# Distances added to the scores by TensorE in the first half of batch 0, in place of mask products, with a new order of steps

## The chip, the cores and the metric

The kernel runs on one core of a Trainium2 chip. A core has a matrix engine (TensorE), VectorE, ScalarE, GpSimd and a queue engine (SyncE, "SP"), which work beside each other and are tied together by semaphores, and 16 DMA engines that all queues share. TensorE writes to PSUM, which has eight banks; the other engines read it from there. The metric is the device time of one execution in microseconds (us). A profile is one execution of its own; its "span" reaches from the first instruction to the last.

## The reference

Attention over 4 batches, 8 heads, 768 positions of 64 values, with 8 global keys and a local band of 96, and distances with a slope for each head as bias; then a gated feed-forward layer over the 3072 tokens:

```python
scores = scale * np.matmul(q, k.transpose(0, 1, 3, 2))
is_global = pos[None, :] < int(n_global)
is_local = (rel >= 0) & (rel < int(n_local))
keep = is_global | is_local
dist = np.where(is_global & ~is_local, float(n_local), np.abs(rel).astype(np.float32))
slopes = 2.0 ** (-8.0 * (np.arange(H, dtype=np.float32) + 1) / H)
bias = -slopes[:, None, None] * dist[None, :, :]
scores = np.where(keep, scores + bias[None, :, :, :], -1000000000.0)
a = np.exp(scores - max); a = a / (sum(a) + 1e-09)
x = np.matmul(a, v)                  # then tokens x 512
g = x @ w_gate
out = (g / (1 + exp(-g)) * (x @ w_val)) @ w_out
```

(The lines are joined and shortened.) `w_gate` and `w_val` are 512 x 1536, `w_out` is 1536 x 512.

## The kernel before

All matrix operands are 16-bit floats; loads on GpSimd's queue narrow them on the way from HBM.

Attention. The keys are cut into 14 chunks of 56, each with the 8 global keys in front (64 rows); a chunk is met by a window of 152 queries. Chunks are packed into "units": in batch 0 units 0 and 1 cover the first 384 queries, units 2 to 4 the second 384; in the other batches five units cover all 768. A unit has two groups of four heads (g = 0, 1); TensorE works on four heads at a time, each in a 64 x 64 quarter of its array. For batch 0, q and k are loaded by halves (`ld_half`, a load of 96 KB each for two head pairs), turned by matmuls with an identity (`tr_half`), and copied out of PSUM (`keys_half`, `queries_half`). Then for each unit and group:

- `scores` (step `c`): k times q into two PSUM banks;
- `exps` (`x`): the exponential, on ScalarE;
- `mask` (`m`): on VectorE, a product with the exponential of slope times distance, which is zero where a key is not to be seen. These masks are made by `make_masks` (`M`) from a small table `dist` of three window patterns.

When the units of a half are ready, `weigh` (`w`) sums the exponentials (part 0) and multiplies them with v (parts 1 and 2); `invert` (`i`) and `spread_r` (`r`) make the reciprocals of the sums, and `scaled` (`p`) writes x, transposed, for 384 tokens, in two sides. Batch 1's q and k come partly by `ld_four` (`L4`) and matmuls (`U`), partly, as in batches 2 and 3, by `ld_rows` (`Lr`), DMA transposes on SP's queue (`tr_dma`, `D`) and copies (`K`).

v is loaded head by head with `ld_v` (`Lv`). In batch 0 each head has two loads, one for chunks 0 to 6 and one for 7 to 12. Batch 0's global rows of v are loaded once (`VG`), narrowed (`Ga`) and copied to every chunk (`Gc`).

Feed-forward. The 3072 tokens are eight blocks of 384. For each block and each of 12 column blocks f: four products with `w_gate` (`g`) and four with `w_val` (`v`), a hyperbolic tangent on ScalarE (`t`), two VectorE steps (`s`, `h`), and then the output products (`o`) with `w_out`, copied out and stored (`e`) through SP's queue. The weights come in pieces of 256 KB (`Lw.which.n.c`: gate or value, four column blocks f, half of the rows).

The order. Nothing is scheduled by a compiler: `ORDER` is a list of some 2,000 steps, written out, and each engine and each queue meets its part of it in that order. `fill.N@bank` are matmuls of ones into an unused bank; they compute nothing. `name@bank` gives the PSUM bank. GpSimd issues nearly all loads and has at most eight in flight.

Of the kernel before, what the change touches and what calls it, by code (L numbers as in the profile page):

```python
# [21 lines left out]
def _build_dist(NG, NL, H):  # L22
# [20 lines left out]
    d = np.concatenate([np.concatenate([d, d]), slopes.reshape(2 * CH, 4)], axis=1)  # L43
# [16 lines left out]
Lw.1.1.1 ga.0.0@0 x.0.1.2 Lv.0.6.7.13 ga.0.1@1 gb.0.1 va.0.1@7 m.0.1.4.V t.0.1 va.0.0@6 Lw.1.1.0  # L60
vb.0.1 Lw.0.2.1 m.0.1.2.V m.0.1.3.V g.0.3@3 x.0.0.2 v.0.3@2 s.0.1 Lw.0.2.0 vb.0.0 v.0.2@4 t.0.3
h.0.1 m.0.0.2.V w.0.1.0@5 Lr.1.1.7 Lr.1.1.5 g.0.4@1 gb.0.0 g.0.2@7 t.0.4 Lr.1.1.1 D.1.3.1 s.0.3
h.0.3 Lr.1.1.3 i.0.1 r.0.1 Lw.1.2.1 L4.0.0 g.0.6@3 LG.1.1 U.2.0@2 s.0.4 U.3.0@5 t.0.0 s.0.0 g.0.7@1
g.0.5@0 t.0.2 s.0.2 Lw.1.2.0 Lo.0 t.0.6 Lr.1.1.4 h.0.0 Lr.1.1.2 h.0.2 s.0.6 w.0.1.1@6 Lr.1.1.6
w.0.1.2@3 kw.3.A t.0.5 v.0.4@5 p.0.1.0 v.0.6@6 LG.3.1 v.0.7@7 h.0.4 v.0.5@5 p.0.1.1 g.1.0@3 h.0.6
g.0.11@4 kw.2.V s.0.5 g.1.1@6 t.1.0 LG.2.1 s.1.0 Lo.1 g.1.4@0 D.1.2.1 h.0.5 g.1.6@2 Lr.1.1.0 Lo.2
t.0.11 t.1.4 Lv.1.2.0.13 Lr.2.0.3 v.1.4@3 g.1.5@5 s.0.11 s.1.4 t.0.7 s.0.7 h.0.7 g.0.10@0 v.1.5@4
t.1.5 t.1.1 s.1.5 h.1.4 s.1.1 v.1.0@1 t.0.10 Lt.2.0 g.1.10@7 h.1.0 U.0.0@3 h.1.5 U.1.0@5 kw.0.V
g.1.9@4 t.1.6 g.1.11@1 v.0.10@6 t.1.10 v.1.2@3 s.1.10 kw.1.V s.0.10 h.0.10 s.1.6 v.0.11@5 h.0.11
t.1.11 v.1.1@7 h.1.1 g.1.3@0 v.1.10@6 g.1.2@7 o.0.1.0@2 h.1.10 s.1.11 v.1.6@5 t.1.3 t.1.9 t.1.2  # L70
g.0.8@6 s.1.2 D.1.1.1 s.1.9 LG.1.0 g.0.9@1 t.0.9 h.1.6 h.1.2 v.0.9@7 LG.3.0 Lt.1.0 Lt.1.1
Lv.1.1.0.13 g.1.8@4 s.1.3 s.0.9 Lv.1.3.0.13 h.0.9 v.1.3@5 v.0.8@3 t.0.8 s.0.8 Lr.3.1.7 Lv.1.6.0.13
c.1.1.0@0 o.0.2.0@7 o.0.1.1 h.0.8 h.1.3 c.1.1.1@5 x.1.1.0 D.1.0.1 x.1.1.1 c.1.1.2@0 x.1.1.2 t.1.8
m.1.1.2.V s.1.8 o.0.1.2 m.1.1.1.V o.0.1.3 e.0.1 o.0.2.1 o.0.2.2 o.0.2.3 o.1.2.0@3 Lv.1.7.0.13
o.0.0.0@5 v.1.11@6 c.1.0.1@0 Lr.2.0.2 Lr.2.1.2 o.0.0.1 Lv.1.4.0.13 Lv.1.5.0.13 Lv.1.0.0.13 e.0.2
g.1.7@2 x.1.0.1 m.1.0.1.V m.1.1.0.V o.0.0.2 v.1.9@4 t.1.7 Lr.2.1.0 s.1.7 o.0.0.3 v.1.8@2 G.1.0 G.1.1
Lv.3.4.0.13 c.1.0.2@0 Lr.2.1.4 x.1.0.2 h.1.11 h.1.9 h.1.8 v.1.7@6 Lr.2.0.4 Lr.2.1.5 o.1.2.1
c.1.0.0@0 h.1.7 e.0.0 o.1.2.2 o.1.2.3 o.1.1.0@7 x.1.0.0 e.1.2 o.1.1.1 m.1.0.0.V o.1.1.2 m.1.0.2.V
o.1.1.3 w.1.0.0@4 Lr.2.0.0 Lr.3.0.0 w.1.0.1@5 w.1.0.2@0 i.1.0 r.1.0 o.1.0.0@2 Lr.3.0.2 p.1.0.1
o.1.0.1 e.1.1 o.1.0.2 Lr.2.1.1 o.1.0.3 e.1.0 c.1.0.4@3 x.1.0.4 c.1.0.3@0 p.1.0.0 c.1.1.4@5 g.2.5@7  # L80
x.1.1.4 x.1.0.3 g.2.0@3 t.2.5 m.1.1.4.V v.2.9@6 t.2.0 s.2.5 m.1.0.3.V g.2.9@0 g.2.2@5 Lr.2.1.3
Lr.2.0.6 v.2.5@4 LG.2.0 t.2.9 s.2.9 h.2.5 Lv.2.7.0.13 c.1.1.3@1 s.2.0 x.1.1.3 m.1.0.4.V m.1.1.3.V
g.2.3@7 Lr.2.0.1 h.2.9 g.2.8@0 v.2.3@4 D.2.0.0 w.1.1.0@2 i.1.1 Lr.2.1.6 g.2.1@3 g.2.7@6 v.2.1@1
t.2.3 s.2.3 D.2.2.1 D.2.1.1 t.2.1 s.2.1 t.2.2 s.2.2 Lv.3.2.0.13 Lt.3.1 h.2.1 Lr.3.1.3 Lr.2.1.7
Lr.2.0.7 g.2.4@7 h.2.3 g.2.6@3 v.2.2@1 r.1.1 D.2.1.0 G.2.1 v.2.0@2 g.2.10@5 t.2.6 Lr.2.0.5 h.2.2
s.2.6 v.2.8@4 v.2.4@3 t.2.4 h.2.0 K.2.0.A t.2.7 s.2.7 s.2.4 h.2.4 v.2.6@1 Lv.2.3.0.13 D.2.2.0
Lr.3.1.4 D.2.3.0 D.2.3.1 w.1.1.1@6 t.2.10 s.2.10 w.1.1.2@2 v.2.10@5 h.2.6 g.2.11@1 t.2.11 p.1.1.1
o.2.0.0@2 o.2.0.1 h.2.10 p.1.1.0 t.2.8 s.2.8 h.2.8 g.3.9@3 g.3.11@5 t.3.11 v.2.7@6 v.2.11@7 s.2.11
g.3.5@0 s.3.11 h.2.7 Lr.3.0.5 K.2.1.A t.3.9 Lv.2.2.0.13 Lv.2.0.0.13 Lv.3.7.0.13 o.2.0.2 t.3.5 h.2.11
Lr.3.1.0 o.2.0.3 v.3.11@4 g.3.7@5 D.2.0.1 o.2.1.0@7 g.3.2@1 o.2.2.0@6 o.2.2.1 K.2.2.A Lt.2.1 s.3.9  # L90
e.2.0 t.3.7 s.3.7 o.2.2.2 h.3.11 K.2.3.V o.2.2.3 t.3.2 s.3.5 c.2.1.2@4 Lr.3.0.1 s.3.2 c.2.0.0@2
c.2.0.1@0 x.2.1.2 e.2.2 Lv.2.5.0.13 Lv.2.1.0.13 m.2.1.2.V o.2.1.1 o.2.1.2 v.3.7@4 h.3.7 x.2.0.0
m.2.0.0.V g.3.0@5 x.2.0.1 o.2.1.3 t.3.0 c.2.1.0@2 x.2.1.0 m.2.1.0.V c.2.1.1@0 v.3.2@4 h.3.2 v.3.5@6
g.3.1@2 e.2.1 v.3.9@3 x.2.1.1 v.3.1@4 Lr.3.0.4 m.2.0.1.V t.3.1 s.3.1 v.3.0@1 h.3.9 Lv.3.3.0.13
g.3.3@0 t.3.3 Lr.3.0.7 Lv.2.6.0.13 g.3.10@7 h.3.5 Lr.3.1.5 s.3.0 c.2.0.2@2 c.2.1.3@5 h.3.1 t.3.10
# [38 lines left out]
def kernel(  # L134
# [95 lines left out]
    def v_of(b):  # L230
        return vSs[b % NV]
# [458 lines left out]
```

## Time and profile before

| what | value |
|---|---|
| device time, three runs | 241.59, 243.34, 243.68 us (median 243.34) |
| profiled execution | 241.13 us, span 239.2 us |
| granted TensorE clock, mean | 0.999 |
| ScalarE busy | 99.7 us (42%) |
| DMA, mean over the span | 106 GB/s |
| loads of `ld_half`, issue to landing, median | 5.6 us (k), 6.1 us (q) |

A line of the timeline reads: start, length, engine, line of the kernel, operation, what is written from what, how many instructions of the kind are merged, and in brackets how long the engine stood idle before and what ended that. Matmuls overlap, so the length of a group is the time from its first start to its last end. In the chain of waits a line has start, length and what the time went to; "issue" is time in which nothing in the profile was waited for. POOL is GpSimd, DVE is VectorE, ACT is ScalarE, PE is TensorE, PEld its weight loads.

### The profile page before, as it was taken

Reading aid. Unit: us, or ns where it says so; the run is one execution under the profiler, and the core shown is the slowest. Engines: PE = TensorE matmul, PEld = TensorE weight load, DVE = VectorE, ACT = ScalarE, POOL = GpSimd, SP = SyncE. Lnnn points to the kernel's source line nnn. Section 1 sums busy time; section 2 is a strip of 40 time slices with the busy share of each in tenths; the row PEclk is TensorE's granted clock in tenths of the full one; section 3 lists DMA queues with packets and bytes.
Section 4 is the critical chain, followed back from the end, with each engine's and each line's share of the span. In section 5 each row is a group of like instructions: output and inputs, shape, how many; then the busy total and the mean of one; then the engine's idle time right before and its main releaser. Section 6 shows DMA issues by size and latency. Waiting matters only on the chain.

```text
span 239.2 us, 7117 instructions
## 1 busy us (share of the span) xinstructions
PE 230.2 (96%) x3048; PEld 133.2 (56%) x3048; DVE 163.4 (68%) x362; ACT 99.7 (42%) x186; POOL 92.2 (39%) x123
## 2 busy tenths in 40 slices
PE   6897989999999999999999999999999999999994
PEld 4665556655445556555555556545665566545643
DVE  7389978987265688853996886894777366634840
ACT  5596443323542534447651328552333223222401
POOL 8798896645699990599800000000000000000000
PEclk9999999999999999999999999999999999999999
DMA  7999999999999999999991680003000210012003
GB/s 99 170 138 167 178 153 182 183 163 183 166 148 184 203 154 154 137 147 155 143 123 47 145 159 9 1 3 123 14 0 0 90 47 0 0 47 88 0 10 125
DMA packets 90767, 25.36 MB, mean 106 GB/s; under 512 B 78336, under 2 KB 87792, under 8 KB 90736
## 3 DMA queue, kind: packets, MB, share of 16 engines
q0 software_dynamic: 70128, 14.21, 68.8%
q1 hardware_dynamic: 20464, 10.58, 22.1%
q8 instruction: 24, 0.39, 0.7%
q10 hardware_dynamic: 144, 0.12, 0.2%
q14 instruction: 7, 0.06, 0.1%
HBM read 28.51 MB, written 6.29 MB: 145 GB/s over the span
## 4 chain that ended last, share of the span: by engine, by line
PE 84%; DMA 8%; POOL 5%; issue 1%; DVE 0%; POOLq 0%
PE PS L582 50%; PE PS L614 27%; PE PS L475 3%; PE PS L538 3%; DMA wg<-in_moe_w_gate_dram 3%; DMA st<-in_q_dram 3%; POOL vS L271 3%; DMA wv<-in_moe_w_val_dram 2%; PE PS L532 1%; POOL st L253 1%; POOL wv L319 1%; POOL wg L319 1%; PE PS L426 0%; DVE osb L623 0%; POOLq L670 0%
## 5 line engine op out<-in xcount | busy, mean ns | idle before, releaser
L588 ACT ACTIVATE th<-PS 128x384 f32<-128x384 f32 x96 | 44.4, 492 | 75.9 <-PE PS L582 70.6
L582 PE MATMUL PS<-xT,wv 128*128 128x384 f16 x384 | 72.4, 326 | 1.4 <-DMA wv<-in_moe_w_val_dram 1.4
L582 PE MATMUL PS<-xT,wg 128*128 128x384 f16 x384 | 73.2, 326 | 0.0
L614 PE MATMUL PS<-wo,hT 128*128 128x512 f16 (+2 forms) x300 | 67.9, 371 | 0.0
L599 DVE TENSOR_TENSOR hT<-PS,sl 128x384 f16<-128x384 f32 x96 | 51.2, 552 | 24.0 <-PE PS L582 22.2
L592 DVE SCALAR_TENSOR_TENSOR sl<-th,PS 128x384 f32<-128x384 f32 x96 | 50.7, 547 | 18.6 <-ACT th L588 17.9
L582 PEld LDWEIGHTS <-wv 128*128 128x128 f16 x384 | 37.1, 98 | 27.7 <-DMA wv<-in_moe_w_val_dram 1.9
L582 PEld LDWEIGHTS <-wg 128*128 128x128 f16 x384 | 36.5, 98 | 25.2 <-issue 0.2
L614 PEld LDWEIGHTS <-hT 128*128 128x128 f16 x300 | 28.0, 98 | 29.3
L484 ACT ACTIVATE at<-PS 128x912 f16<-128x912 f32 (+1 forms) x40 | 32.0, 829 | 20.8 <-PE PS L475 20.7
L271 POOL DMA_DIRECT2D vS<-in_v_dram x40 | 32.9, 834 | 8.4 <-DMA wo<-in_moe_w_out_dram 2.3
L505 DVE TENSOR_TENSOR at<-at,masks 128x912 f16<-128x912 f16 (+5 forms) x56 | 22.6, 442 | 13.0 <-ACT at L484 13.0
L629 ACT ACTIVATE osb<-PS 128x512 f32<-128x512 f32 (+1 forms) x24 | 14.2, 593 | 34.1 <-PE PS L614 31.6
L312 POOL DMA_DIRECT2D st<-in_q_dram x24 | 21.1, 885 | 1.5 <-DMA wv<-in_moe_w_val_dram 1.5
L312 POOL DMA_DIRECT2D st<-in_k_dram x16 | 13.9, 896 | 8.9 <-DMA kN<-st 8.8
L567 DVE TENSOR_TENSOR xT<-PS,rb 128x768 f16<-128x768 f32 x16 | 14.9, 951 | 1.8 <-PE PS L538 1.2
L475 PE MATMUL PS<-qT,kT 64*64 64x152 f16 (+4 forms) x464 | 12.4, 225 | 1.8 <-issue 1.0
L475 PEld LDWEIGHTS <-kT 64*64 64x64 f16 x464 | 8.0, 106 | 7.8 <-issue 6.4
L538 PEld LDWEIGHTS <-vS 64*32 64x32 f16 x1024 | 9.3, 90 | 3.4 <-issue 2.9
L538 PE MATMUL PS<-at,vS 64*32 64x152 f16 (+4 forms) x1024 | 10.5, 218 | 0.0
L358 PE MATMUL PS<-ones 128*128 128x256 f16 x44 | 8.8, 366 | 1.2 <-DVE ones L334 1.2
L556 DVE STREAM_TRANSPOSE rb<-dR 128x768 f32<-128x768 f32 x8 | 7.8, 976 | 0.2
(49 smaller groups left out, 95.9 us busy)
## 6 DMA issues: line engine op xcount, KB each, us to landing
out_dram<-osb SPq DMA_DIRECT2D x23, 256.0 KB, 2.5
st<-in_q_dram POOLq DMA_DIRECT2D x24, 96.0 KB, 6.1
vS<-in_v_dram POOLq DMA_DIRECT2D x24, 91.0 KB, 4.9
wv<-in_moe_w_val_dram POOLq DMA_DIRECT2D x6, 256.0 KB, 6.2
wg<-in_moe_w_gate_dram POOLq DMA_DIRECT2D x6, 256.0 KB, 6.5
wo<-in_moe_w_out_dram POOLq DMA_DIRECT2D x3, 512.0 KB, 10.0
st<-in_k_dram POOLq DMA_DIRECT2D x16, 96.0 KB, 5.6
st<-in_k_dram POOLq DMA_DIRECT2D x4, 192.0 KB, 6.5
```

Of the source, the lines that this page charges most:

```text
L271: nc.gpsimd.dma_start(out=v_of(b)[CH * c + NG:CH * c + CH, c0:c1, j, :], in_=v[b, h, KC * c0:KC * c1, :].rearrange("(i p) d -> p i d", p=KC))
L312: nc.gpsimd.dma_start(out=stage(b, i, h % 2, True)[:, h // 4, :, h // 2 % 2, :], in_=KQ[i][b, h].rearrange("(t p) d -> p t d", p=128))
L475: nc.tensor.matmul(PS[64 * e:64 * e + 64, bank + hi, col:col + n], lhsT=kT_of(b, hp)[r, CH * c:CH * c + CH], rhs=qTs[b, hp][r, q0:q0 + n], ...
L484: nc.scalar.activation(out=at[:, :, 0:w], in_=PS[:, bank:bank + 2, 0:w], func=AF.Exp, scale=scale)
L505: ENG[e].tensor_mul(a2, a2, m2)
L538: nc.tensor.matmul(PS[r, bank + e, o:o + n], lhsT=V[s, c, j, what - 1::2], rhs=at[s, hi, col:col + n], start=first, stop=last, skip_group_ ...
L567: nc.vector.tensor_mul(x_of(2 * b + half)[:, side::2, :], PS[:, bank:bank + 2, 0:TB], rbs[b, half])
L582: nc.tensor.matmul(PS[:, bank, 0:TB], lhsT=w[:, c, 128 * f:128 * f + 128], rhs=xTs[t][:, c, :], start=(c == SIDES[0]), stop=(c == SIDES[-1]))
L588: nc.scalar.activation(out=th, in_=PS[:, gv[t, f, 0], 0:TB], func=AF.Tanh, scale=0.5)
L592: nc.vector.scalar_tensor_tensor(out=sl, in0=gv[t, f, "t"], scalar=1.0, in1=PS[:, gv[t, f, 0], 0:TB], op0=AluOp.add, op1=AluOp.mult)
L599: nc.vector.tensor_mul(hTs[t, f // 3][:, f % 3, :], PS[:, gv[t, f, 1], 0:TB], gv[t, f, "s"])
L614: nc.tensor.matmul(PS[:, bank, 0:c.stop - c.start], lhsT=hTs[t, f // 3][:, f % 3, 128 * i:128 * i + 128], rhs=wo[:, f, c], start=(f == 0), ...
```

## The change

In units 0 and 1 of batch 0, for both groups, the mask step goes. In its place `biases` (step `b`) runs on TensorE ahead of the scores: the left operand is a 64 x 64 diagonal that holds minus the slope of a head times 8 (the root of 64, which the scale in the exponential takes out again), the right operand the table of distances, and the scores are then accumulated on top, without a fresh start. `make_diagonals` (`Zs`) makes the four diagonals on VectorE from the table, which is longer by 4 slopes and 64 columns of an identity. All other units keep their masks.

```diff
+    def make_diagonals():
+        nc.vector.tensor_mul(
+            diag, dist[:, MW + 8:].unsqueeze(1).broadcast_to([128, 4, CH]),
+            dist[:, MW + 4:MW + 8].unsqueeze(2).broadcast_to([128, 4, CH]))
...
     def fill(bank, n):
-        for _ in range(n):
-            nc.tensor.matmul(PS[:, bank, 0:256], lhsT=ones[:, 0:128], rhs=ones[:, 0:256],
-                             start=True, stop=True)
+        twice = ones[:, :].unsqueeze(1).broadcast_to([128, 2, 256])
+        for _ in range(n // 2):
+            nc.tensor.matmul(PS[:, bank, :], lhsT=ones[:, 0:128], rhs=twice, start=True, stop=True)
...
+    def biases(bank, b, g, u):
+        at_bank["c", b, g, u] = bank
+        for k, (col, n, x, w0) in enumerate(side_by_side(b, u)):
+            for hi in range(2):
+                r = slice(64 * hi, 64 * hi + 64)
+                m0 = WIN * x + w0
+                near = dist[r, m0:min(m0 + n, MW)]
+                if m0 + n > MW:
+                    near = near.unsqueeze(1).broadcast_to([CH, n // WIN, WIN])
+                for e in range(2):
+                    nc.tensor.matmul(
+                        PS[64 * e:64 * e + 64, bank + hi, col:col + n],
+                        lhsT=diag[r, 2 * g + e, :], rhs=near, start=k == 0, stop=False,
+                        skip_group_check=True)
```

`side_by_side` is the part of `mask` that joins windows which lie side by side, now a function of its own. `scores` takes no bank where biases came first, and starts with `start=not biased`.

On VectorE, narrowing and copying the global rows of v is no longer a copy but the maximum of a row with itself; on ScalarE it stays a copy. Of the four `Gc` copies three were on VectorE and one on ScalarE; now two are on each.

```diff
-        copy_on(e)(out=first16[r, :], in_=first[r, :])
+        if e == "V":
+            nc.vector.tensor_tensor(out=first16[r, :], in0=first[r, :], in1=first[r, :], op=AluOp.max)
+        else:
+            nc.scalar.copy(out=first16[r, :], in_=first[r, :])
```

`ORDER` is new from the first step to the last. Its beginning, before:

```
pre VG.S.1 Li.S VG.S.0 Z.1 Z.2 Lh.0.1.2.4 fill.2@3 fill.2@3 fill.2@0 Ld.A fill.2@1 Z.0 Ga.0.A Ga.1.V
M.1 M.3 fill.2@7 fill.4@2 Lh.1.0.0.2 Lh.0.0.0.2 Gc.0.1.V Lh.1.0.2.4 Lh.0.0.2.4 Lh.1.1.0.2 fill.4@3
M.0 Gc.1.1.A Gc.1.0.V T.1.0.1@4 Lh.0.1.0.2 fill.2@5 fill.4@2 Lv.0.5.0.7 Y.0.0.0 Gc.0.0.V fill.4@6
```

and after:

```
pre Y.0.0.0 Lh.0.0.2.4 fill.2@7 fill.2@0 fill.2@1 fill.2@1 Ld.S Zs b.0.1.0@2 Lh.1.0.2.4 Z.1 VG.A.1
fill.2@1 fill.4@4 fill.4@5 Z.0 Ga.1.A Li.S VG.S.0 M.3 fill.4@5 Lh.0.0.0.2 T.3.0.0@6 T.3.0.1@5
T.2.0.1@4 T.2.0.0@1 Lh.1.0.0.2 Lh.1.1.0.2 fill.2@7 fill.4@0 k.3.0.A q.3.0.A k.2.0.V q.2.0.A c.0.1.0
```

The first loads on GpSimd's queue, in order. Before: eight of q and k, the eight first-half loads of v and two weight pieces are the first 18. After: seven of q and k, a v load, the last of q and k, one batch-1 row load, five v loads, a gate piece, a second-half v load, a gate piece, and the last two first-half v loads are the first 20. The diagonals' table is loaded first on SP's queue (before: on ScalarE's), and one of the two loads of global rows moves to ScalarE's queue. The products on the first tokens begin in both orders after all ten score units of batch 0 and the three weighing parts of its first half:

```
... w.0.0.2@2 Lv.0.4.7.13 p.0.0.1 c.0.0.3@4 ga.0.1@7 Lv.0.6.7.13 ga.0.0@6 m.0.1.2.V g.0.3@1 gb.0.0
gb.0.1 ... g.0.2@0 ... va.0.0@2 ... vb.0.0 va.0.1@4 ... vb.0.1 g.0.5@3 g.0.6@5 ... w.0.1.0@1 ... v.0.3@7
```

(after; some steps left out). The scores of batch 2 (`c.2.1.0`) come, after, behind 288 products and 102 output matmuls from the first product on; before (`c.2.1.2`) behind 312 and 99.

235 lines of the change are left out of this document (124 added, 111 removed).

## The prediction

> **What bounds the kernel now.** I read the page first, then the chain of waits in order of time, then the timelines of TensorE, GpSimd and VectorE over the first 45 us. The page, with the span, the engines and the DMA share by slices:
>
> ```profile
> span 239.2 us, 7117 instructions
> PE 230.2 (96%) x3048; PEld 133.2 (56%) x3048; DVE 163.4 (68%) x362; ACT 99.7 (42%) x186; POOL 92.2 (39%) x123
> DMA  7999999999999999999991680003000210012003
> ```
>
> TensorE is busy nearly always, and the DMA engines are full from 6 us to about 126 us (a slice is 6 us). The chain of waits (start, length, what) tells which of the two decides where:
>
> ```profile
> 10.21 0.28 issue
> ...
> 18.75 6.97 DMA wg<-in_moe_w_gate_dram
> ...
> 29.43 5.95 DMA wv<-in_moe_w_val_dram
> ...
> 35.43 9.92 PE PS L582 x60
> ...
> 182.18 5.18 PE PS L614 x24
> ...
> 218.01 10.40 PE PS L582 x64
> ```
>
> Up to 35.4 us the chain runs over GpSimd issues and DMA landings; after that it is TensorE alone, with no gap, to the end. So the time is: when TensorE gets its first feed-forward product, plus the waits after that, plus a fixed amount of matmuls (10.40/64 = 0.1625 us for one product, 5.18/24 = 0.216 for one output matmul). TensorE around that point:
>
> ```profile
> 18.20 0.93 PE L532 MATMUL PS<-at,ones 128*32 128x152 f16 x28
> 19.05 0.39 PE L475 MATMUL PS<-qT,kT 64*64 64x152 f16 x12
> 19.37 0.65 PE L538 MATMUL PS<-at,vS 64*32 64x152 f16 x56
> 21.20 0.18 PE L475 MATMUL PS<-qT,kT 64*64 64x40 f16 x1 [0.99 <-issue]
> 22.89 1.15 PE L582 MATMUL PS<-xT,wg 128*128 128x384 f16 x6
> 24.51 0.99 PE L582 MATMUL PS<-xT,wv 128*128 128x384 f16 x5 [0.31 <-DMA wv<-in_moe_w_val_dram]
> 35.43 2.77 PE L582 MATMUL PS<-xT,wv 128*128 128x384 f16 x16 [1.08 <-DMA wv<-in_moe_w_val_dram]
> ```
>
> The first product starts at 22.89 us, and afterwards TensorE waits 0.31 + 1.08 = 1.39 us for weights. Ahead of the first product stand, before and after the change alike, the same things: all ten score units of batch 0 and the three weighing steps of its first half. So everything from the first product on is the same list of matmuls in another order, and the change can move the span only by the start of that product and by the waits behind it.
>
> **The change: masks against biases.** Removed are the mask products of four units, which on VectorE were 3 + 4 + 1 instructions:
>
> ```profile
> 13.81 0.76 DVE L505 TENSOR_TENSOR at<-at,masks 128x608 f16<-128x608 f16 x3
> 15.55 1.30 DVE L505 TENSOR_TENSOR at<-at,masks 128x912 f16<-128x912 f16 x4
> 17.86 0.63 DVE L505 TENSOR_TENSOR at<-at,masks 128x912 f16<-128x912 f16 x1 [0.40 <-ACT at L484]
> 21.55 1.81 DVE L567 TENSOR_TENSOR xT<-PS,rb 128x768 f16<-128x768 f32 x2
> ```
>
> That is 2.69 us of VectorE, of which only the last, 0.63 us, stands between the last exponential and the weighing at 18.20. Added are 32 bias matmuls (one run of 456 columns and three of 304, 104 and 48, four array quarters, two groups; 7,296 columns) and one VectorE product for the diagonals. No row shows such a matmul. The fill matmuls bound it:
>
> ```profile
> 1.19 4.02 PE L358 MATMUL PS<-ones 128*128 128x256 f16 x18 [1.19 <-DVE ones L334]
> 6.64 2.31 PE L358 MATMUL PS<-ones 128*128 128x256 f16 x10
> 12.10 0.61 PE L358 MATMUL PS<-ones 128*128 128x256 f16 x4
> ```
>
> Early fills start 0.21 us apart for 256 columns, later ones 0.11. One after another 7,296 columns would be 6.1 us at the slow pace, 3.1 at the fast one; the score matmuls at 19.05 (12 in 0.39, four quarters at a time) are the nearer row and give a quarter of it, 0.8 to 1.5 us. I take zero on the path, because they stand where the fills stand now, in waits for q and k; the fills go from 44 of 256 columns to 27 of 512. If that cover is gone, they cost the 0.8 to 1.5.
>
> **The change: the order of loads, which decides.** The weighing at 19.37 needs the eight first-half v loads. GpSimd's timeline (start, length; in brackets the idle time before and what ended it):
>
> ```profile
> 10.49 0.71 POOL L253 DMA_DIRECT2D st<-in_q_dram  x1 [0.73 <-DMA st<-in_q_dram]
> 13.54 2.32 POOL L271 DMA_DIRECT2D vS<-in_v_dram  x3 [0.27 <-DMA st<-in_k_dram]
> 15.86 1.48 POOL L319 DMA_DIRECT2D wg<-in_moe_w_gate_dram  x2
> 21.88 0.71 POOL L271 DMA_DIRECT2D vS<-in_v_dram  x1 [0.36 <-DMA wg<-in_moe_w_gate_dram]
> 23.12 0.69 POOL L271 DMA_DIRECT2D vS<-in_v_dram  x1 [0.53 <-DMA wg<-in_moe_w_gate_dram]
> 24.74 0.64 POOL L277 DMA_DIRECT2D vS<-in_v_dram  x1 [0.24 <-DMA wv<-in_moe_w_val_dram]
> ```
>
> GpSimd has eight loads in flight: the 12th issue, at 10.49, waits for the 4th landing (10.21 in the chain, 0.28 earlier), the 15th at 13.54 for the 7th. From 10.49 to 13.54 three loads of q or k landed: 1.02 us each. The issues at 21.88 and 23.12 wait for two weight loads in a row, the 18th and 19th: 1.24 each. At 24.74 the 21st has landed, 1.62 later, with one v load between: 0.37 for that. Batch 1's rows (Lr) are 768 pieces against 392 of a first-half v load: estimate 0.37 x 768/392 = 0.72.
>
> Before, the first 18 loads are 8 of q and k, the 8 v loads and 2 weights, and the 18th has landed at 21.88 - 0.28 = 21.6. After, the last first-half v load is the 20th: the same 18 loads' worth, one batch-1 row load (0.72) and one second-half v load (0.37) more. By that row it lands at 21.6 + 1.09 = 22.7. That is the upper end. The lower: the first seven loads are of the same kind as before, and the 7th landed at 13.26; then 0.37 + 1.02 + 0.72 + 5 x 0.37 + 1.24 + 0.37 + 1.24 + 2 x 0.37 = 7.6 gives 20.8, if none of the irregular delay between the 7th and 18th landing comes back. I take 22.4, near the end that is itself a row. Before, this landing was over by 19.37. So the v loads come about 3 us later and swallow what the mask's absence and the earlier first-half q load (4th instead of 5th load, 1.02 us) free: the weighing of values now waits for v, not for scores.
>
> From that landing, L, to the first product: weighing 0.65 us, then VectorE scales the first side (1.81/2, about 0.95), or on TensorE 8 scores, the second weighing and 12 scores (0.2 + 0.65 + 0.35): about L + 1.85, because inversion and spreading of the sums now come ahead. First product at 24.25 against 22.89: **+1.36 us** (22.65 to 24.55: -0.24 to +1.66).
>
> Waits behind it. Counting on from L = 22.4 with the prices above: the value weights' first half, the 25th load, lands at 26.7, and TensorE comes to it after 16 products at 26.85; the 27th at 28.1 against 28.15; the 30th at 31.0 against 32.05; the last second-half v load at 32.8 against 34.0; the 37th at 35.3 against 36.75. Two of these are even to 0.15 us. I take 0.3 us of waits in place of 1.39: **-1.1 us**; the range is 0 to 1.4. The loads before went v first and weights later, so these waits are what the new order buys with the later v.
>
> **The change: other moves.** Rows of VectorE and ScalarE for the distances and the global rows of v:
>
> ```profile
> 2.85 0.17 DVE L341 CAST slope<-dist 128x4 f32<-128x4 f16 x1 [0.73 <-DMA dist<-dist_c]
> 3.62 3.17 DVE L297 COPY vS<-first 8x1792 f16<-8x1792 f16 x3
> 6.16 1.68 ACT L297 COPY vS<-first 8x1792 f16<-8x1792 f16 x1
> ```
>
> The diagonals need the distances, now on SP's queue ahead of the identity and one of the two global-row loads (the other goes on ScalarE's queue); their landing stays near 2.8 us, when the slope copy starts. Copies of the global rows of v (8x1792) become one 1.07 us VectorE step fewer and one 1.68 us ScalarE step more, and VectorE's are a maximum of a row with itself. No row shows that form; the mask product (912 in 0.63) scales to 1.2 us, the scaling out of PSUM (768 in 0.95) to 2.2. Both end before v lands, so I take nothing.
>
> Behind the first product the order of 2,000 steps is new. The tightest place that I find is the scores of batch 2, which follow the last of eight DMA transposes on SP:
>
> ```profile
> 94.82 4.91 SPq L447 DMA_TRANSPOSE qT<-st  x2
> 108.04 0.79 PE L475 MATMUL PS<-qT,kT 64*64 64x152 f16 x36
> DMA to landing us min/median/max: 2.6/7.3/8.4
> ```
>
> The eighth is issued near 97.5 and lands, at the median, at 104.8; TensorE came at 108.04. After, TensorE comes to the first such scores with 24 products, one weighing less and 3 output matmuls more behind it: 108.04 - 22.89 - 1.39 = 83.8, less 3.9, less 0.7, plus 0.65 is 79.8; from 24.25 with 0.3 of waits, 104.4. Landing and need coincide: **+0.4 us** for the median landing, zero to 2.2.
>
> **Sum**: 1.36 - 1.1 + 0.4 = +0.66 us. The profiled execution took 241.13 us around its span of 239.2; the median of the three runs is 243.34 (241.59 to 243.68). So 241.8 for a run like the profiled one, and 244.0 on the median.
>
> **Rivals.** *Loads come earlier, faster.* The third load was late, as GpSimd's issues show.
>
> ```profile
> 2.79 0.68 POOL L253 DMA_DIRECT2D st<-in_k_dram  x1
> 3.45 0.68 POOL L253 DMA_DIRECT2D st<-in_q_dram  x1
> 9.00 0.76 POOL L271 DMA_DIRECT2D vS<-in_v_dram  x1 [0.59 <-DMA st<-in_k_dram]
> ```
>
> It landed at 9.00 - 0.28 = 8.7, 1.5 us before the fourth where 1.02 is usual, and 5.9 us after its issue at 2.79, while VectorE copied from 3.62 to 6.79 (the row above). If such copies held up the loads, the new order, without copies of that kind, gets up to 1.5 us back; with the lower end of L (-1.6), 0.66 - 1.5 - 1.6 = -2.4 us: 240.9. Against it: GpSimd's issues stay 0.66 us apart through the copies. [...]
>
> *The transposes, slower.* If the eighth takes the 8.4 us maximum from an issue 0.7 later, it lands at 106.6: 2.2 us of wait instead of 0.4, +2.5 in all: 245.8. It decides as soon as the landing passes 104.4. For it speaks that all later work stands behind these scores on TensorE; against it, that the eight transposes may be issued earlier as well.
>
> *The clock falls.* Between the first weighing, near 17 us, and the last v load TensorE has fills of 14 x 256 columns (1.5 us at the later pace) and 52 score matmuls (1.6) for a wait of some 5: a gap near 2 us. Before, its longest gap there was 0.99 us. If the pace falls back to the early fills' half, 3.5 us of products cost 1.75 more: +2.4, 245.7. [...]
>
> *No mask effect at all* is my forecast's own mechanism: masks leave VectorE, and v ends the wait.
>
> **How the numbers follow.** One per cent, 2.4 us, is about what a measurement can tell from none. Forecast 0.5; earlier loads 0.2; transposes 0.2; clock and unseen waits 0.1. Low end: the first rival's 240.9 less 0.5 for where three runs lie, 240.4. High end: the second's 245.8, 1.1 for waits for weights at their upper bound, and 0.6 for the runs, 247.5. Faster 0.2, same 0.5, slower 0.3.
>
> **What would show it.** First product between 22.7 and 24.6 us, with the weighing of values just ahead ended by a v load; under 0.5 us of waits for weights until 37 us; the third load landing near 8.7 or, for the first rival, near 7.2; the wait of the first batch-2 scores near 104 us. Wrong would be a v load landing by 20 us, or a wait over 1 us on TensorE after 37.

## The result, and the profile after

Twenty executions of each kernel: 241.41 us median after (239.66 to 243.94), 242.28 before (240.62 to 244.35), a ratio of **0.9955 (0.9934 to 0.9976)**: 0.45% faster. Two repetitions gave 0.9964 (0.9939 to 0.9989) and 0.9981 (0.9951 to 1.0010); the kernel before against itself gave 0.9982 (0.9952 to 1.0013), so the gain is not much more than what two sets of executions of one kernel differ by. The ratios leave out executions more than 1.5% above the fastest of their kernel, the medians don't. Within 1%, as the likeliest case had it, but to the other side: the forecast was 0.66 us slower, the measurement is about 0.9 us faster. (`ORDER` has 1,010 steps before and 1,015 after; the texts above say some 2,000.)

The page after: span, engines, granted clock of TensorE and DMA share by slices, and one DMA queue (packets, MB, share).

```profile
span 240.7 us, 7145 instructions
PE 231.2 (96%) x3063; PEld 131.0 (54%) x3063; DVE 156.2 (65%) x346; ACT 105.2 (44%) x195; POOL 92.3 (38%) x123
PEclk9979999999999999999999999999999999999999
DMA  6999999999999994999998450021001200021003
q8 instruction: 24, 0.39, 0.7%
```

TensorE has 15 pairs of weight load and product more (32 biases, 17 fills fewer), VectorE 7.2 us less work. Note queue q8, which the prediction did not look at: 24 packets of 16 KB. TensorE's timeline after:

```profile
18.48 0.58 PE L577 MATMUL PS<-at,ones 128*32 128x152 f16 x28 [0.66 <-DVE kT L415]
22.73 0.65 PE L583 MATMUL PS<-at,vS 64*32 64x152 f16 x56 [0.69 <-DMA vS<-in_v_dram]
24.48 2.77 PE L627 MATMUL PS<-xT,wg 128*128 128x384 f16 x16
28.85 1.47 PE L627 MATMUL PS<-xT,wv 128*128 128x384 f16 x8 [1.61 <-DMA wv<-in_moe_w_val_dram]
```

A v load ends the wait of the weighing of values, the first product starts at 24.48 and a wait for value weights follows: the steps of the prediction, nearly at its times. Yet this profiled execution took 242.52 us and that of before 241.13: these two stand the other way round than the medians. So more executions of both were profiled. The trace gives the start of the first product and of the last matmul:

| execution | time | first product | last matmul |
|---|---|---|---|
| before | 241.13 | 22.89 | 236.00 |
| before_again | 241.49 | 24.56 | 236.29 |
| before_2 | 242.05 | 24.47 | 236.92 |
| before_3 | 242.44 | 23.73 | 237.30 |
| after | 242.52 | 24.48 | 237.55 |
| after_again | 240.61 | 23.52 | 235.64 |
| after_2 | 241.23 | 23.74 | 236.25 |
| after_3 | 241.19 | 24.35 | 236.21 |

The forecast's base, 22.89, is by 0.84 us the earliest of before's four first products. The mean of after's four is 24.02, where 24.25 was forecast; that of before's four is 23.91. From the first product to the last matmul before takes 212.7 us on average and after 212.4.

### The profile page after: what moved, and what is told of

It reads as the page before. It is cut to its first block, busy times and chain, and to the rows that moved or that the text cites. A ratio compares the mean times of both kernels' runs of the same rounds, so it can differ in the third digit from the quotient of the medians.

```text
span 240.7 us, 7145 instructions
## 1 busy us (share of the span) xinstructions
PE 231.2 (96%) x3063; PEld 131.0 (54%) x3063; DVE 156.2 (65%) x346; ACT 105.2 (44%) x195; POOL 92.3 (38%) x123
## 4 chain that ended last, share of the span: by engine, by line
PE 86%; DMA 7%; POOL 5%; issue 1%; DVE 0%; POOLq 0%
PE PS L627 51%; PE PS L659 26%; DMA st<-in_k_dram 4%; PE PS L583 4%; PE PS L530 3%; DMA wg<-in_moe_w_gate_dram 3%; POOL st L262 2%; PE PS L577 2%; POOL vS L280 2%; POOL wg L335 1%; PE PS L447 1%; POOL wv L335 1%; POOL vS L286 1%; DVE osb L668 0%; POOLq L715 0%
## 5 line engine op out<-in xcount | busy, mean ns | idle before, releaser
L627 PE MATMUL PS<-xT,wv 128*128 128x384 f16 x384 | 71.4, 326 | 1.6 <-DMA wv<-in_moe_w_val_dram 1.6
L627 PE MATMUL PS<-xT,wg 128*128 128x384 f16 x384 | 70.9, 326 | 0.1
L659 PE MATMUL PS<-wo,hT 128*128 128x512 f16 (+2 forms) x300 | 66.1, 371 | 0.0
L627 PEld LDWEIGHTS <-wg 128*128 128x128 f16 x384 | 37.1, 98 | 26.0 <-DMA wg<-in_moe_w_gate_dram 0.6
L627 PEld LDWEIGHTS <-wv 128*128 128x128 f16 x384 | 36.6, 98 | 26.7 <-DMA wv<-in_moe_w_val_dram 2.0
L550 DVE TENSOR_TENSOR at<-at,masks 128x912 f16<-128x912 f16 (+5 forms) x48 | 19.8, 450 | 10.0 <-ACT at L539 9.9
L328 POOL DMA_DIRECT2D st<-in_q_dram x24 | 20.6, 870 | 12.5 <-DMA kN<-st 11.5
L380 PE MATMUL PS<-ones 128*128 128x512 f16 x27 | 9.8, 486 | 1.2 <-DVE wg L340 1.2
```

The lines of the kernel that those rows point to most:

```text
L328: nc.gpsimd.dma_start(out=stage(b, i, h % 2, True)[:, h // 4, :, h // 2 % 2, :], in_=KQ[i][b, h].rearrange("(t p) d -> p t d", p=128))
L550: ENG[e].tensor_mul(a2, a2, m2)
L627: nc.tensor.matmul(PS[:, bank, 0:TB], lhsT=w[:, c, 128 * f:128 * f + 128], rhs=xTs[t][:, c, :], start=(c == SIDES[0]), stop=(c == SIDES[-1]))
L659: nc.tensor.matmul(PS[:, bank, 0:c.stop - c.start], lhsT=hTs[t, f // 3][:, f % 3, 128 * i:128 * i + 128], rhs=wo[:, f, c], start=(f == 0), ...
```

## The experiments

All ratios are to runs of the kernel before on the same chip, with a 95% interval.

**Repetitions, and the two halves of the change.** before_again and after_again are the two kernels unchanged. after_masks has the order after, with masks in place of the biases in units 0 and 1:

```diff
-  b.0.1.1@5 c.0.1.1 ... x.0.1.0 x.0.1.1
+  c.0.1.1@5 ... x.0.1.0 m.0.1.0.V x.0.1.1 m.0.1.1.V
```

and the same for the other units, with `M.2` and `M.1` (two of the masks) made earlier. before_biases is the opposite: order, fills and copies as before, biases for masks:

```diff
-  c.0.0.1@6 ... m.0.0.1.V
+  b.0.0.1@6 c.0.0.1
```

> The kernel before, unchanged, for a second profile. If its first profile was an ordinary execution, the first product starts again near 22.9 us, with 1.4 to 1.7 us of waits for weights behind it. If that execution was a lucky one (241.13 us against a median of 242.28), start and waits together come about 1.1 us later. Ratio to before 1.000 within 0.3%.

> The changed kernel, unchanged, for a second profile. If its first profile (242.52 us, median 241.41) was an unlucky execution, the first product and the waits behind it together come about 1.1 us earlier than there (24.48 us and 2.0 us). If the order of steps behind the first product gave the gain, they don't, and the span differs later. Ratio to before 0.993 to 0.998.

> After's order with mask products in units 0 and 1 of batch 0 and no biases. Theory loads (the v loads end the wait, the bias is swallowed): the last first-half v load lands near 22.7 us as in after, the first product within 0.3 us of it, ratio to after within 0.2%. Theory masks (the biases are what gains): 0.6 to 1.5 us later, ratio to after 1.003 to 1.006, with the first weighing of values ended by VectorE and not by a v load.

> Before's order, fills and copies, with the biases in place of the masks of units 0 and 1. Theory loads: the v loads land near 18.9 us, what is freed on VectorE (0.6 us at the last mask) is worth at most 0.5 us; the bias matmuls right ahead of the scores cost 0.4 to 1.5; ratio to before 0.998 to 1.004. Theory masks: 0.6 to 1.5 us faster, ratio 0.994 to 0.997.

Measured: before_again 0.9982 (0.9952 to 1.0013), after_again 0.9964, after_masks 1.0016 (0.9986 to 1.0046), and before_biases **1.0408** (1.0349 to 1.0467), some 10 us slower by the ratio. Nothing of the forecast explains that. The two repetitions: before_again started its first product at 24.56, with 0.30 us of waits for weights behind it, 0.6 us later in sum than the first profile, between both cases of its expectation; after_again's start and waits together came 1.8 us earlier than after's, more than the 1.1 expected of an unlucky first profile. after_masks is taken up below. TensorE's timeline of before_biases, whose profiled execution, 255.97 us, was the longest of six:

```profile
16.67 0.22 PE L520 MATMUL PS<-qT,kT 64*64 64x152 f16 x1 [0.98 <-issue]
22.87 0.54 PE L573 MATMUL PS<-at,vS 64*32 64x152 f16 x25 [2.16 <-issue]
43.22 4.32 PE L617 MATMUL PS<-xT,wv 128*128 128x384 f16 x13 [4.51 <-issue]
109.91 0.87 PE L649 MATMUL PS<-wo,hT 128*128 128x512 f16 x3 [2.04 <-issue]
```

TensorE stands still in the middle of a list of matmuls, and "issue" says that nothing in the profile was waited for: no data, no bank, no engine. Counted by TensorE's matmuls, these four stops come ahead of numbers 224, 352, 736 and 1504: each is 96 plus a multiple of 128. And by the trace's packets, one of queue q8's 16 KB lands 1.25 to 1.57 us before each of them. A packet is thus taken to hold 128 pairs of weight load and product (an estimate: the four numbers lie 128, 384 and 768 apart, and in before 24 packets stand against 3,048 pairs, 127 each), and TensorE to stop where the next packet hasn't landed. The traces of before and after fit this: matmuls 224, 352, 480 and so on to 3040 start behind the landing of the first packet, the second and so on, by 1.35 to 23.3 us in before and by 2.40 to 24.9 in after, in none of the 23 cases ahead of it. Two shorter stops of this trace, 0.40 us ahead of 480 and 0.77 ahead of 1887, also follow a landing, by 1.21 and 1.48 us; 1887 is one short of the count, and why isn't shown. The 0.99 us at 21.20 in the prediction's own fence is of the same kind: it stands ahead of matmul 352, 1.35 us after a landing.

**Is it the number of instructions?** before_pad32 leaves masks and arithmetic of before alone and adds 32 products of 8 columns at the places of the biases. before_biases_fewer is before_biases with the fills of the kernel after, 22 fewer instruction pairs for the same columns. after_fills256 gives the kernel after the fills of before, 27 pairs more.

```diff
+    def pad(bank):
+        for e in range(8):
+            nc.tensor.matmul(PS[:, bank, 0:8], lhsT=ones[:, 0:128], rhs=ones[:, 0:8], start=True, stop=True)
```

```diff
-        for _ in range(n // 2):
-            nc.tensor.matmul(PS[:, bank, :], lhsT=ones[:, 0:128], rhs=twice, start=True, stop=True)
+        for _ in range(n):
+            nc.tensor.matmul(PS[:, bank, 0:256], lhsT=ones[:, 0:128], rhs=ones[:, 0:256], start=True, stop=True)
```

(the last is after_fills256; before_biases_fewer is its reverse)

> The kernel before, masks and all, with 32 extra TensorE products of 8 columns that compute nothing: eight ahead of each of the four scores of units 0 and 1, where the biases stand in before_biases. They add 32 weight loads and 32 products of a few tens of ns, 1 us of TensorE at most, in stretches where it waits. Instruction theory (TensorE's instructions come in 16 KB packets, one for 128 pairs of weight load and product, and TensorE stops where it runs ahead of them; 32 pairs more put other stretches across the packets' ends): idle time of TensorE ended by issue of 2 to 5 us in a row near 33 to 43 us, as in before_biases, and again near 97 and 110; 246 to 254 us, ratio 1.015 to 1.05. Work theory (before_biases lost its 11.5 us by what the biases themselves cost, or by masks that go): 242 to 243.5 us, ratio under 1.005.

> before_biases (the order before, biases ahead of the scores of units 0 and 1, no masks there) with the fills of the kernel after: 22 products of 512 columns in place of 44 of 256, so that TensorE has 10 pairs of instructions more than before instead of 32. Instruction theory: by the starts of TensorE's matmuls in the profile of before, stretches of 128 pairs shifted by 10 take 3.8 us near 20 us, and no other under 5.4 us until 70; stalls of 1 to 2 us in all near 20 us, and most of the 11.5 us of before_biases goes: 242 to 245 us, ratio 0.999 to 1.012. Work theory: the biases stand at the same places and the fills have the same columns, so it stays at 252 to 255, ratio 1.04.

> The kernel after with the fills of the kernel before: each product of 512 columns is two of 256 again, 54 instead of 27, so 27 pairs of instructions more and the same columns. Instruction theory: stretches of 128 pairs shifted by 27 take 1.5 us near 24 us and 3.8 us near 40 us in the profile of after, where 5.4 us go without a stall; 4 and 1.6 us of idle time ended by issue there, more later: 245 to 251 us, ratio 1.01 to 1.035. Work theory: as after, 241.4, ratio 0.996.

Measured: before_pad32 **1.0296** (1.0241 to 1.0352), before_biases_fewer **1.0011** (0.9978 to 1.0043), after_fills256 **1.0096** (1.0055 to 1.0137). The first two are as the count of instructions had it, the third lies just under its range (1.01). TensorE's timelines, before_pad32 first (its profiled execution, 254.87 us, was the longest of six):

```profile
29.54 0.97 PE L583 MATMUL PS<-xT,wv 128*128 128x384 f16 x5 [1.26 <-issue]
44.02 4.32 PE L583 MATMUL PS<-xT,wv 128*128 128x384 f16 x13 [4.19 <-issue]
110.23 0.82 PE L615 MATMUL PS<-wo,hT 128*128 128x512 f16 x3 [1.59 <-issue]
```

before_biases_fewer:

```profile
23.35 0.20 PE L573 MATMUL PS<-at,vS 64*32 64x48 f16 x3 [1.64 <-issue]
40.56 1.95 PE L617 MATMUL PS<-xT,wg 128*128 128x384 f16 x11 [0.60 <-issue]
```

after_fills256:

```profile
24.52 0.26 PE L530 MATMUL PS<-qT,kT 64*64 64x152 f16 x3 [0.49 <-issue]
40.83 1.31 PE L627 MATMUL PS<-xT,wg 128*128 128x384 f16 x7 [1.98 <-issue]
```

Thirty-two products that do nothing cost 7 us by the ratio. They push a weighing of 144 small products (1.36 us in all) to matmuls 589 to 732, so that the packet from 608 to 735 is used up almost wholly within it; the stop of 4.19 us stands right behind, as the one of 4.51 in before_biases, where the count is the same. Taking 22 pairs out brings before_biases back to the time of before. Each of the stops shown stands ahead of 96 plus a multiple of 128 again (two later ones, of 0.86 and 0.63 us, are one and three short of it, like that at 1887 right behind a landing). Where the stops fell in before_biases_fewer was not all foreseen (none was expected at 40), and after_fills256 lost less near 24 us than the 4 expected: TensorE waits 1.35 us for a v load there anyhow, ahead of 22.28, and the stop ahead of 24.52 is 0.49 us.

**Masks by themselves.** after_masks differs from after in masks and in 32 instruction pairs. after_masks_pad keeps the pairs: the biases are computed, then overwritten.

```diff
-                        rhs=qTs[b, hp][r, q0:q0 + n], start=not biased, stop=True,
+                        rhs=qTs[b, hp][r, q0:q0 + n], start=True, stop=True,
```

> after_masks with TensorE's stream of the kernel after, product for product: the biases are computed into the banks as in after, but the scores then start afresh and overwrite them, and the mask products of units 0 and 1 run on VectorE as in after_masks. Two causes are open for the 1.2 us between after_masks (ratio 1.0016) and after (0.9955 and 0.9964). If masks on VectorE stand in the way of the first weighing or of copies that TensorE waits for: 242.3 to 242.8, ratio 1.000 to 1.003. If it was TensorE's stream (32 products fewer, so other packets of instructions and more time at half clock, 1.9 stretches of 3.4 us on average against 0.4): as after, 241.2 to 241.6, ratio 0.995 to 0.998, and mostly one such stretch or none.

Measured 0.9986 (0.9957 to 1.0014), between both expectations; the split isn't settled. By its time after_masks is where the masks would put it, 1.2 us over after_again on the same chip in the medians. TensorE in after_masks, and then in after_masks_pad:

```profile
18.30 0.95 PE L574 MATMUL PS<-at,ones 128*32 128x152 f16 x28 [1.80 <-DVE kT L412]
25.20 2.77 PE L624 MATMUL PS<-xT,wg 128*128 128x384 f16 x16
104.56 0.39 PE L527 MATMUL PS<-qT,kT 64*64 64x152 f16 x12 [0.49 <-DMA qT<-st]
```

```profile
23.32 0.65 PE L580 MATMUL PS<-at,vS 64*32 64x152 f16 x56
25.21 2.77 PE L624 MATMUL PS<-xT,wg 128*128 128x384 f16 x16
```

With masks the first product comes at 25.2, 1.2 us after the mean of after; but no wait for value weights follows, and the last matmul starts at 236.64 and 236.38, against 236.41 on average in after. In these two executions, then, what the masks delay the weights behind would have delayed too; that doesn't explain the 1.2 us of the medians. Of these some 0.3 lie outside the span (device time less span is 2.16 us in the median of after_masks, 1.82 in after_again), from no cause that is shown.

**Copies.** before_max has VectorE's maximum form instead of copies, after_copies the reverse.

```diff
-        copy_on(e)(out=first16[r, :], in_=first[r, :])
+        nc.vector.tensor_tensor(out=first16[r, :], in0=first[r, :], in1=first[r, :], op=AluOp.max)
```

> The kernel before with the maximum form in place of VectorE's copies of the global rows of v, nothing else. First rival: the third load lands near 7.2 us instead of 8.7 and all that follows comes up to 1.5 us earlier: 240.8 to 241.5, ratio 0.993 to 0.997. Other theory: third load between 7.9 and 9.7 as in the other traces, time as before, ratio 0.998 to 1.002.

> The kernel after with VectorE's global rows of v copied, as before, instead of the maximum of a row with itself. First rival of the prediction (VectorE copies hold up loads): the copies stand near 10 to 20 us here, and the loads under way there come later, the last first-half v load with them, by up to 1.5 us: 242 to 243, ratio 0.999 to 1.003. Other theory (the third load comes late with and without copies, 7.9 to 9.7 us in the traces so far, and nothing of it hangs on VectorE): as after, 241.4, ratio 0.994 to 0.998.

Measured: before_max 1.0000 (0.9964 to 1.0036), after_copies 0.9975 (0.9947 to 1.0003). VectorE and GpSimd of before_max, and the same of after:

```profile
3.52 3.19 DVE L304 TENSOR_TENSOR vS<-first 8x1792 f16<-8x1792 f16 x3
9.58 0.76 POOL L271 DMA_DIRECT2D vS<-in_v_dram  x1 [1.18 <-DMA st<-in_k_dram]
```

```profile
7.23 0.28 DVE L420 CAST kT<-PS 128x112 f16<-128x112 f32 x1 [3.09 <-ACT kT L415]
9.81 0.78 POOL L280 DMA_DIRECT2D vS<-in_v_dram  x1 [1.39 <-DMA st<-in_k_dram]
```

The issue that waits for the third load comes at 9.58 and 9.81 (9.00 in before): the load is as late with the maximum in place of copies, and with VectorE idle for 3.09 us. The forms take the same time, too: 3.19 us for three against 3.17.

The profiled execution of before_max, 244.82 us and one of its longest, also happened on the longest stop ahead of matmul 352:

```profile
24.22 0.19 PE L482 MATMUL PS<-qT,kT 64*64 64x40 f16 x1 [3.73 <-issue]
24.34 0.96 PE L545 MATMUL PS<-at,vS 64*32 64x152 f16 x56
26.17 2.10 PE L589 MATMUL PS<-xT,wg 128*128 128x384 f16 x6
```

After it 56 weighings take 0.96 us instead of 0.65 and six products 2.10 instead of 1.15: TensorE comes out of this stop at a slower pace. The granted clock shows it: 0.50 from 23.73 to 30.56 us, from within the stop on.

**The fills.** after_small_fills keeps their number and makes them 8 columns wide.

```diff
-            nc.tensor.matmul(PS[:, bank, :], lhsT=ones[:, 0:128], rhs=twice, start=True, stop=True)
+            nc.tensor.matmul(PS[:, bank, 0:8], lhsT=ones[:, 0:128], rhs=ones[:, 0:8], start=True, stop=True)
```

> The kernel after with its 27 fills at 8 columns instead of 512: the same number of TensorE instructions, hardly any work in them. The fills compute nothing, so by work theory nothing changes: ratio 0.995 to 0.998. Third rival of the prediction (TensorE falls to half pace in gaps that the fills cover): more stretches at half clock, a granted clock of 0.98 to 0.985 instead of 0.993 to 1.0, products at half pace for 3.4 to 7 us more: 243 to 246, ratio 1.003 to 1.015.

Measured 1.0007 (0.9975 to 1.0039), between both expectations: 0.6 to 1.3 us more than after by the ratios of after's three sets (0.9955 to 0.9981), with intervals that overlap in part. TensorE:

```profile
17.83 0.95 PE L577 MATMUL PS<-at,ones 128*32 128x152 f16 x28 [0.48 <-DVE kT L415]
22.08 0.96 PE L583 MATMUL PS<-at,vS 64*32 64x152 f16 x56 [1.00 <-DMA vS<-in_v_dram]
24.65 3.66 PE L627 MATMUL PS<-xT,wg 128*128 128x384 f16 x16
```

The weighings take 0.95 and 0.96 us instead of 0.58 and 0.65, 16 products 3.66 instead of 2.77. The granted clock expected at 0.98 to 0.985 is 1.0 in this run all the same, and that number misleads: the trace's record of the clock begins at 26.49 us here (at 5.39 in after), and the page counts the time ahead of it as full (9 in all 40 slices). The rows up to 26.49 show the slower pace throughout.

**An earlier v.** after_v_first brings the last two first-half v loads forward, ahead of a row load of batch 1, a second-half v load and a gate piece, and after_v_w puts the first two value pieces ahead of a gate piece besides.

```diff
-  q.1.0.A Lr.1.1.4 Lv.0.6.0.7 ... Lv.0.7.0.7 ... Lv.0.0.7.13 ... Lw.0.1.1 ... Lv.0.3.0.7 Lv.0.0.0.7
+  q.1.0.A Lv.0.6.0.7 ... Lv.0.7.0.7 Lv.0.3.0.7 Lv.0.0.0.7 ... Lw.0.1.1 Lv.0.0.7.13 ... Lw.0.1.0 Lr.1.1.4
```

> The kernel after with its load order changed at one place: the last two first-half v loads right behind the sixth, one row load of batch 1, one second-half v load and one gate piece behind them instead of ahead. Work theory: the last first-half v load lands at 19.5 to 20.5 us instead of 21.7 to 22.7, the weighing of values waits for nothing or for scores, the first product comes 0.8 to 1.5 us earlier, the waits for weights behind it grow by up to 0.5: 240.2 to 241.2, ratio 0.991 to 0.996. Instruction theory: in after, 128 pairs of instructions up to the first product take 6.0 to 6.1 us, and they would take about 5 with v earlier, where before stopped for 0.99 and 1.20 us: idle time ended by issue of about 1 us near 21 us takes the gain back: as after, 0.995 to 0.998.

> after_v_first with the two first value pieces one place earlier, ahead of the second gate piece: work theory: they land 1.25 us earlier, near 24.1 and 25.4 us, TensorE's wait for them (1.46 us in after_v_first) falls to 0 to 0.4, and the gate piece behind them lands near 26.6, before the products on it come; 239.6 to 240.6, ratio 0.988 to 0.992. Rival: TensorE, earlier by that much, waits for the next pieces instead, at 28 to 34 us: as after_v_first, 0.993 to 0.996.

> The kernel after, to stand beside after_v_first_2 on one chip: ratio to before 0.994 to 0.998, in its profile no stop at the 352nd pair, a first product at 23.5 to 24.5 us with a v load just ahead, then 0.5 to 1.8 us of wait for value weights.

> after_v_first once more beside after_3. If the landing of v decides the end: 0.6 to 1.2 us below after_3, ratio to before 0.990 to 0.994. If the loads of weights behind it take most of it back (1.46 us of wait for value weights in its first profile, against 0.6 to 1.6 in after's): 0 to 0.5 us below after_3, ratio 0.993 to 0.997, and intervals that overlap.

Measured: after_v_first 0.9939 (0.9912 to 0.9965), after_v_w 0.9977 (0.9943 to 1.0012); then side by side after_3 0.9981 (0.9951 to 1.0010) and after_v_first_2 0.9986 (0.9955 to 1.0017). TensorE of after_v_first:

```profile
20.53 0.65 PE L579 MATMUL PS<-at,vS 64*32 64x152 f16 x56
22.42 2.77 PE L623 MATMUL PS<-xT,wg 128*128 128x384 f16 x16
26.65 1.47 PE L623 MATMUL PS<-xT,wv 128*128 128x384 f16 x8 [1.46 <-DMA wv<-in_moe_w_val_dram]
```

and of after_v_w:

```profile
28.62 1.47 PE L623 MATMUL PS<-xT,wg 128*128 128x384 f16 x8 [1.88 <-DMA wg<-in_moe_w_gate_dram]
```

The first product comes 1.6 us earlier than the mean of after, and TensorE then waits 1.46 us for value weights, or 1.88 for gate weights where those come later. So the loads set the pace at this place, and what one of them gains another loses. after_v_w and the second set of after_v_first lie above all that was expected of them (0.988 to 0.996 and 0.990 to 0.997). No version here is shown to beat after.

**More executions.** before_2, before_3 and after_2 are the two kernels once more, one profiled execution each.

> One more execution of the kernel before, profiled. If stops for instructions make its median longer than its first profile: TensorE idle, ended by issue, at its 352nd pair of weight load and product, for 1 to 4 us, ahead of the first product, and the time follows first product plus waits. If not: no such stop, or under 1 us, in an execution of 242 us or more.

> As before_2, another execution of the same kernel: a stop of 1 to 4 us at the 352nd pair if instructions are the cause, first product at 22.9 to 26.2 us; otherwise none.

> One more execution of the kernel after, profiled. If instructions are the cause: no idle time ended by issue on TensorE (its 352nd pair is needed 5.5 to 6.5 us after the 224th, and the packet is there by then), first product at 23.5 to 24.5 us, then a wait of 0.5 to 1.8 us for value weights. If not: a stop at the 352nd pair here too.

Their times stand in the table above. TensorE of before_2, and then of before_3:

```profile
22.55 0.18 PE L475 MATMUL PS<-qT,kT 64*64 64x40 f16 x1 [0.77 <-issue]
36.25 2.77 PE L582 MATMUL PS<-xT,wv 128*128 128x384 f16 x16 [0.57 <-DMA wv<-in_moe_w_val_dram]
```

```profile
23.40 0.40 PE L475 MATMUL PS<-qT,kT 64*64 64x48 f16 x16 [1.14 <-DVE xT L567]
34.81 1.23 PE L538 MATMUL PS<-at,vS 64*32 64x152 f16 x123 [0.70 <-DMA vS<-in_v_dram]
46.69 0.87 PE L426 MATMUL PS<-ident,st 96*64 96x96 f16 x32 [0.70 <-DMA st<-in_k_dram]
```

Neither bears out that the stop makes before's executions long: in before_2, at 242.05 us, it is 0.77 us, under the 1 to 4 that were expected, and before_3 has hardly a stop; its 242.44 us come with waits for VectorE, v and k. after_2 came as expected. The stops ahead of matmul 352, by matmul starts and packets of the trace (us):

| execution | 224 to 351 takes | packet lands, after 224 | 351 to 352 |
|---|---|---|---|
| before | 3.76 | 3.58 | 1.17 |
| before_again | 3.76 | 3.79 | 1.37 |
| before_2 | 3.76 | 3.33 | 0.95 |
| before_3 | 3.76 | 2.80 | 0.27 |
| before_max | 2.56 | 4.91 | 3.91 |
| after | 6.10 | 2.63 | 0.01 |
| after_again | 6.01 | 3.35 | 0.01 |
| after_2 | 6.52 | 2.77 | 0.01 |
| after_3 | 5.98 | 2.37 | 0.00 |
| after_copies | 6.06 | 4.50 | 0.01 |

In all ten rows matmul 352 starts at the later of its turn and 1.2 to 1.6 us after the packet's landing. In the order before its turn comes first; in the order after, which waits for v between 224 and 352, the packet was there in time in all five (in after_copies just so).

## Why the prediction was right or wrong

**Landing of the last first-half v load: right.** 22.4 was forecast (20.8 to 22.7); the trace has 22.69, 21.73, 21.95 and 22.56 in the four profiles of after, and v ends the wait in each, as in after_again:

```profile
21.77 0.65 PE L583 MATMUL PS<-at,vS 64*32 64x152 f16 x56 [0.60 <-DMA vS<-in_v_dram]
26.61 1.47 PE L627 MATMUL PS<-xT,wv 128*128 128x384 f16 x8 [0.34 <-DMA wv<-in_moe_w_val_dram]
28.48 1.47 PE L627 MATMUL PS<-xT,wg 128*128 128x384 f16 x8 [0.39 <-DMA wg<-in_moe_w_gate_dram]
```

**"First product at 24.25 instead of 22.89": right in the first number, wrong in the second.** After's mean is 24.02; before's is 23.91, so the shift of 1.36 us is 0.1. This is the step that failed: the forecast took one execution for what is fixed, and that one was early. The other three profiles of before start at 24.25 on average, the very value forecast for after. What made it early lies ahead of the stop: matmul 224 started at 16.27 us, and at 17.94, 17.84 and 17.11 in before_again, before_2 and before_3, where a load of k or q came later; in the same order:

```profile
9.70 0.70 PE L382 MATMUL PS<-ident,st 96*64 96x96 f16 x24 [1.45 <-DMA st<-in_k_dram]
9.66 0.70 PE L382 MATMUL PS<-ident,st 96*64 96x96 f16 x24 [1.66 <-DMA st<-in_k_dram]
7.03 0.36 PE L382 MATMUL PS<-ident,st 96*64 96x96 f16 x8 [2.39 <-DMA st<-in_q_dram]
```

(The first profile waited 0.96 us for the same q load and not for that k load.) These three also have a stretch of 3.41 us at a granted clock of 0.50 ahead of matmul 224 (from 12.71, 12.64 and 7.32 us); in the first the record of the clock begins at 10.23 us and shows none. How much each of the two costs isn't separated. The stop of 0.99 us, which the prediction saw as a gap and not as a wait for instructions, varies too: 0.27 to 1.37 us between matmuls 351 and 352 in the four profiles of before, and the new order covers it. It isn't what made the first profile early; its 1.17 is the second longest of the four.

**"Waits for weights 0.3 us": mis-sized.** The first value piece alone makes TensorE wait 1.61, 0.34, 0.63 and 0.66 us in the four profiles of after, 0.8 on average, and a gate piece 0.39 more in one of the fences above. The two landings "even to 0.15 us" were no margin against loads that vary by 1 us. Against that, the 1.39 of before was high: its four profiles wait 1.39, 0.30, 0.76 and 0.38 us for weights, 0.7 on average, after's four 1.0 with the gate pieces. The term of -1.1 us is +0.3.

**Biases at zero: right where they stand, and wrong as a rule.** In the order before, with fills to cover their columns there too, they made a kernel 4% slower, for the most part by their count, as 32 empty products cost 3% and 22 pairs fewer took all of it away: the step priced columns and never instructions. In after 17 fills fewer pay for more than half of them, and the page shows no stop.

**Transposes +0.4: zero in the four profiles of after,** 0.49 in after_masks and, by TensorE's timeline, 0.87 in after_copies:

```profile
104.69 0.39 PE L524 MATMUL PS<-qT,kT 64*64 64x152 f16 x12 [0.87 <-DMA qT<-st]
```

Landing and need do coincide, on either side; the slow case of that rival (2.2 us) didn't come.

**The rivals.** Earlier loads by other copies: fallen, with before_max at 1.0000 and after_copies at 0.9975; with the maximum in place of the copies the issue behind the third load came at 9.58 us instead of 9.00, no earlier, and the copies took as long as the maximum (3.17 and 3.19 us for three). The pace of TensorE: with the wide fills it holds from the first weighing on (28 in 0.58 us, then 16 products in 2.77); without them the slower pace is real, at a price of about 1 us at most. Earlier, from 12.21 to 15.63 us, the clock was 0.50 in after's profile too, with no idle time of TensorE over 0.50 us in as long a stretch before (from 8.79 us on), and after the wait of 1.61 us ahead of 28.85 it stayed at 1.0: here a fall came without the gap near 2 us that this rival counted on.

**From the profile to the median.** The forecast for a run like the profiled one, 241.8, is 0.5 us above after's median over 44 executions, 241.31. To reach 244.0 the prediction added the distance between before's profile and the median of three runs. Of it 1.2 us was those three: before's median over 133 executions is 242.14. The other 1.0 us is what typical executions of before hold beyond its profile, and after doesn't hold the same. A part of it is seen in the granted clock: it is under 0.988 in 38 of these 133 executions (median 242.96, the other 95 have 241.87) and in 2 of after's 44 (the other 42: 241.28). So 0.6 of the 0.83 us between the two medians remains among executions of like clock. That 241.41 lies inside the range is luck: its low end was made for earlier loads, and those didn't come.

What isn't shown is the cause of the 0.9 us. The three terms as measured, +0.1, +0.3 and 0, make after 0.4 us slower, yet its last matmul starts 0.2 us earlier on average. The 0.6 us between the two lie behind the first product, where the prediction had the same list of matmuls with no wait but those for weights and transposes: before_3 waits 0.70 us for v and 0.70 for k there. No run took the stops out of the kernel before and left the rest; four profiles of each kernel scatter by 1.3 and 1.9 us in the last matmul, too much to add up a difference of that size.

## What to carry to other kernels

Count instructions, not only their work: where an engine runs through many small ones, set its stops by "issue" in mid-list against their number and against the packets of the instruction queue. Here TensorE's recurred ahead of 96 plus a multiple of 128, 1.2 to 1.6 us behind a packet, and are read as waits for instructions; 32 pairs more cost 7 us (before_pad32), and 22 fewer took a ratio of 1.0408 down to 1.0011 (before_biases_fewer). So an edit that changes the count is tested against one that changes the count alone. And a forecast of under 1% needs several profiled executions of the kernel before: the one taken as the base here had its first product 1.0 us ahead of the mean of four, more than the whole change that was forecast.

## What the runs showed of the hardware

The traces of before and after have 24 packets of 16 KB each on the queue that the page calls instruction; 128 pairs of weight load and matmul for one is an estimate from where TensorE's stops stand (ahead of 224, 352, 736 and 1504 in before_biases). In the table of ten executions above one packet landed 2.4 to 4.9 us after matmul 224 had started, with the DMA engines busy to 90% or more by each page, and where TensorE had stopped, it went on 1.2 to 1.6 us after the landing. The longest stop was 4.51 us (before_biases), and 32 idle products of 8 columns made a kernel 2.96% slower (before_pad32). After a stop of 3.73 us six products took 2.10 us instead of 1.15, at a granted clock of 0.50 for 6.83 us (before_max). A maximum of 8x1792 16-bit values with themselves took as long as their copy on VectorE (3.19 us for three in before_max, 3.17 in before).
